# Recurrent attention and MLP mixer on one core: last-row decays by small transfers, batch 0 loaded by SP, state parts behind scores, last outputs kept in PSUM, and a new instruction order

## The chip, the cores and the metric

The kernel runs on one core of a Trainium2 chip. A core has TensorE (PE, matmuls, its weight loads shown as PEld), VectorE (DVE), ScalarE (ACT), GpSimd (POOL) and SyncE (SP), each with its own program in order. Loads and stores are issued by POOL (software queue, which can also change the type) or by SP (hardware queue), and move on 16 DMA engines that both share. The time is in device microseconds, the median of several executions; lower is better.

## The reference

Four batches, eight heads, 768 positions, head size 48. First a gated recurrence (no softmax), then an MLP mixer over tokens and over channels:

```python
f = 1.0 / (1.0 + np.exp(-f_logit))
for t in range(S):
    state = f[:, :, t, :, None] * state + einsum('bhd,bhe->bhde', k[:, :, t], v[:, :, t])
    y[:, :, t] = einsum('bhd,bhde->bhe', q[:, :, t], state)
x = y.transpose(0, 2, 1, 3).reshape(B, S, H * D)          # 4 x 768 x 384
h = np.maximum(x.transpose(0, 2, 1) @ w_tok1, 0.0) @ w_tok2   # 768 -> 256 -> 768
u = x + h.transpose(0, 2, 1)
out = u + np.maximum(u @ w_ch1, 0.0) @ w_ch2               # 384 -> 1536 -> 384
```

## The kernel before

**Staging.** A batch's 768 positions are six chunks of 128 (b is the batch, c the chunk). All inputs are turned to bf16 except f. Batch 0 is loaded chunk by chunk: f by SP, and k, q and v by POOL, which casts (`load`, L265). Behind them POOL loads the weights (L272), then batch 1 (f whole, k, q and v by chunk, with w_ch2 after chunk 1), then batches 2 and 3 whole.

**Recurrence of a chunk** (`gates`, `attention`). ACT makes L = ln(1 + exp(-f)) in f_sb (L335, L336), copies it to bf16 as Lhi (L337), and DVE or POOL takes the rest, Llo = L - Lhi (L340, L343). PE sums L over the positions with a triangular matrix (L363, L364), and, but for the last chunk, the whole chunk's sum per channel in eight one-column matmuls (L361, L362). ACT makes G = exp(-sum), Gi = exp(sum) and, from the one-column sums, glast, the decay over the whole chunk, with channels on the partitions (L372, L374, L377). DVE makes qh = q G and kh = k Gi (L380, L382). PE transposes both (L393), DVE copies them to qkT (L397). PE makes the scores per head, 48 rows of the array at a time (L407), DVE multiplies by the triangle into AmT (L414). PE makes the state's parts, kh times v, 64 columns of the array at a time (L430); DVE adds them to the state (L437, L440) and multiplies by glast (L442); ACT or POOL copies it to state_bd in bf16. The chunk's output y is qkT times the state of the chunk before (L459) plus AmT times v (L466), in one PSUM bank; it is copied out as x_bf and x_nat (L322, L324). G, Gi, qh, kh, qkT, AmT, glast and state_bd have two buffers, by c mod 2.

**Mixer of a batch** (`mixer`). tok1 (L491) contracts over all six chunks of x_bf, a relu makes h1T (L495), tok2 (L503) gives h, DVE adds it to x_nat (L507), ACT casts to u_bf, PE transposes (L519), DVE copies to uT (L524). Then ch1 (L535) with a relu to zT on ACT or DVE (L545, L547), ch2 (L557), an add (L563), and a store by SP (L566).

**Order.** `Plan` holds every step with its engine or engines, what it needs and makes, its PSUM bank (eight banks, given out by the plan) and a cost. `order` goes through them as a list scheduler: the step that can start first is next, ties by a rank written out by hand (`due`, `ranks`), and the engine is chosen there where a step names two. In gaps of PE over 700 ns before 24 us it puts matmuls on a constant tile (`idle`, L597) that nobody reads. The program of each engine is then fixed.

## Time and profile before

| | |
|---|---|
| time, three runs | 188.21 us median, 187.18 to 188.94 |
| the profiled execution | 187.83 us, its span 186.0 us |
| mean granted TensorE clock | 0.963 |
| loads and stores | 19.95 MB in 88437 packets, mean 107 GB/s |
| software queue, hardware queue | 78720 packets, 92.0% of 16 engines' span; 9696 packets, 11.0% |
| one-column matmuls L361, L362 | x80 and x80 |
| Lhi copies on ACT, L337 | 12.2 us, x24, 522 ns each |
| DVE: AmT, qkT, qh, kh | 682, 684, 350, 352 ns each |
| POOL: issue of a load of a chunk | 0.9 us, x36 by chunk |

The span runs from the first to the last instruction. Engines overlap, so busy times don't add up to it. The page cuts the span in 40 slices and gives each engine's busy share in tenths; PEclk is the share of TensorE's clock that was granted. A busy time of PE counts matmuls that overlap in its pipeline once, while the mean of one is its own duration; what a matmul costs PE is the time from its start to the next start.

### The profile page before, as it was taken

What the parts mean: (1) busy time and instruction counts of PE and PEld (TensorE: products, weight loads), DVE (VectorE), ACT (ScalarE), POOL (GpSimd) and SP (SyncE); (2) the same over time, 40 slices, a digit from 0 to 9 for tenths busy, and PEclk for the clock granted to TensorE, in tenths of its full rate; (3) what the DMA queues carried; (4) which work ended last, traced back from release to release, by engine and by line L of the source; (5) the groups of instructions that cost most, each with busy time, mean ns of one, the idle gap of its engine ahead of it and who ended that gap; (6) DMA issues with size and microseconds to landing.
All of it is one profiled execution on the core that took longest, in us unless ns stands there. A gap on an engine that the chain in (4) does not pass through costs nothing.

```text
span 186.0 us, 4513 instructions
## 1 busy us (share of the span) xinstructions
PE 175.5 (94%) x1783; PEld 110.5 (59%) x1783; DVE 130.1 (70%) x296; ACT 127.1 (68%) x309; POOL 66.0 (35%) x78
## 2 busy tenths in 40 slices
PE   6879896899999999999999999999999999999992
PEld 2347573556666656666665666666666666665660
DVE  5388885849998999999988848867686628300222
ACT  5799865699974499999999836557874116698000
POOL 7999993275692444504621501011011000000000
PEclk9995559999999999999999999999999999999999
DMA  8999999999999999999991211011000121110132
GB/s 104 138 169 153 162 210 247 185 159 196 142 118 249 179 162 169 247 201 105 79 125 5 81 49 42 4 42 48 0 0 5 65 73 34 42 42 0 46 127 85
DMA packets 88437, 19.95 MB, mean 107 GB/s; under 512 B 81152, under 2 KB 87600, under 8 KB 88416
## 3 DMA queue, kind: packets, MB, share of 16 engines
q0 software_dynamic: 78720, 13.77, 92.0%
q1 hardware_dynamic: 9696, 5.90, 11.0%
q8 instruction: 14, 0.23, 0.6%
q14 instruction: 7, 0.06, 0.1%
HBM read 25.17 MB, written 4.72 MB: 161 GB/s over the span
## 4 chain that ended last, share of the span: by engine, by line
PE 81%; POOL 5%; DMA 4%; ACT 4%; DVE 3%; issue 2%; POOLq 0%; DVEq 0%
PE ps L535 26%; PE ps L557 25%; PE ps L393 5%; PE ps L491 4%; PE ps L407 4%; DMA v_sb<-in_v_dram 4%; PE ps L503 3%; PE ps L466 2%; PE ps L430 2%; PE ps L519 2%; POOL q_sb L265 2%; PE ps L363 2%; ACT u_bf L322 2%; PE ps L364 1%; PE ps L459 1%
## 5 line engine op out<-in xcount | busy, mean ns | idle before, releaser
L557 PE MATMUL ps<-w_ch,zT 128*128 128x384 bf16 x288 | 54.1, 326 | 0.0
L535 PE MATMUL ps<-uT,w_ch 128*128 128x384 bf16 x288 | 52.6, 326 | 0.0
L545 ACT ACTIVATE zT<-ps 128x384 bf16<-128x384 f32 x76 | 36.5, 490 | 8.3 <-PE ps L535 7.9
L557 PEld LDWEIGHTS <-zT 128*128 128x128 bf16 x288 | 26.8, 98 | 16.5
L535 PEld LDWEIGHTS <-w_ch 128*128 128x128 bf16 x288 | 26.3, 98 | 15.9
L414 DVE TENSOR_TENSOR AmT<-ps,tri_bf 128x512 bf16<-128x512 f32 x48 | 30.6, 682 | 5.3 <-PE ps L407 5.2
L563 DVE TENSOR_TENSOR x_nat<-x_nat,ps 128x384 f32<-128x384 f32 x24 | 13.2, 550 | 22.9 <-PE ps L557 22.5
L265 POOL DMA_DIRECT2D q_sb<-in_q_dram x14 | 15.3, 1095 | 13.6 <-issue 5.2
L322 ACT ACTIVATE x_bf<-ps 128x384 bf16<-128x384 f32 x20 | 9.9, 495 | 12.3 <-PE ps L466 12.1
L265 POOL DMA_DIRECT2D k_sb<-in_k_dram x14 | 15.5, 1105 | 7.6 <-DMA f_sb<-in_f_logit_dram 4.5
L397 DVE COPY qkT<-ps 128x1024 bf16<-128x1024 bf16 x24 | 16.3, 684 | 0.7 <-PE ps L393 0.7
L372 ACT ACTIVATE G<-ps 128x384 bf16<-128x384 f32 x24 | 11.8, 490 | 7.3 <-PE ps L364 7.2
L265 POOL DMA_DIRECT2D v_sb<-in_v_dram x14 | 15.4, 1099 | 3.8 <-issue 2.4
L507 DVE TENSOR_TENSOR x_nat<-x_nat,ps 128x384 f32<-128x384 f32 x24 | 11.5, 547 | 4.1 <-PE ps L503 4.1
L322 ACT ACTIVATE u_bf<-x_nat 128x384 bf16<-128x384 f32 x24 | 11.4, 522 | 4.1 <-DVE x_nat L507 4.1
L326 POOL CAST state_bd<-state 48x192 bf16<-48x192 f32 x10 | 3.4, 344 | 29.8 <-DVE state L442 24.3
L335 ACT ACTIVATE f_sb<-f_sb 128x384 f32<-128x384 f32 x24 | 12.0, 523 | 2.7 <-DMA f_sb<-in_f_logit_dram 2.6
L547 DVE TENSOR_SCALAR zT<-ps 128x384 bf16<-128x384 f32 x20 | 10.4, 552 | 3.7 <-PE ps L535 3.6
L322 ACT ACTIVATE state_bd<-state 48x192 bf16<-48x192 f32 x30 | 10.8, 360 | 3.0 <-DVE state L442 2.6
L491 PE MATMUL ps<-x_bf,w_tok 128*128 128x384 bf16 x48 | 11.9, 330 | 1.0 <-ACT x_bf L322 1.0
L337 ACT ACTIVATE Lhi<-f_sb 128x384 bf16<-128x384 f32 x24 | 12.2, 522 | 0.3
L336 ACT ACTIVATE f_sb<-f_sb 128x384 f32<-128x384 f32 x24 | 12.1, 521 | 0.2
(61 smaller groups left out, 275.8 us busy)
## 6 DMA issues: line engine op xcount, KB each, us to landing
out_dram<-x_nat SPq DMA_DIRECT2D x24, 192.0 KB, 1.9
f_sb<-in_f_logit_dram POOLq DMA_DIRECT2D x3, 1152.0 KB, 10.8
f_sb<-in_f_logit_dram SPq DMA_DIRECT2D x6, 192.0 KB, 4.0
k_sb<-in_k_dram POOLq DMA_DIRECT2D x12, 96.0 KB, 6.6
q_sb<-in_q_dram POOLq DMA_DIRECT2D x12, 96.0 KB, 6.1
v_sb<-in_v_dram POOLq DMA_DIRECT2D x12, 96.0 KB, 6.1
w_ch<-in_moe_w_ch_dram POOLq DMA_DIRECT2D x2, 576.0 KB, 10.4
w_ch<-in_moe_w_ch_dram POOLq DMA_DIRECT2D x1, 1152.0 KB, 14.9
```

The costliest lines, as they stand in the source:

```text
L265: add(engine, 0.0, lambda eng=eng, into=into, of=of: eng.dma_start(out=into, in_=of), make=[(n, b % NB, j) for j in (range(NCH) if c is No ...
L322: nc.scalar.activation(out_, in_, AF.Copy, bias=0.0, scale=1.0)
L335: add(ACT, r, lambda: nc.scalar.activation(fb, fb, AF.Exp, bias=0.0, scale=-1.0), make=[key], kind=el)
L336: add(ACT, r, lambda: nc.scalar.activation(fb, fb, AF.Ln, bias=1.0, scale=1.0), make=[key], kind=el)
L337: add(ACT, r, lambda: nc.scalar.activation(hi, fb, AF.Copy, bias=0.0, scale=1.0), need=[key], make=[lk], kind=el)
L397: add(DVE, r, lambda: nc.vector.tensor_copy(qkT[i], turned()), make=[("qkT", i)], bank=p_t, kind=("el", 1024, True, 2))
L414: add(DVE, r, lambda p=p: nc.vector.tensor_tensor(AmT[i][:, 4 * p:4 * p + 4, :], banks[p_a[p].at].rearrange("s (hp t) -> s hp t", t=C), tb ...
L491: add(PE, rank("tok1", rt), lambda rt=rt, kt=kt, pm=pm: nc.tensor.matmul(banks[pm.at][:, 0:DM], lhsT=w_tok1[:, kt, rt * 128:(rt + 1) * 128 ...
L535: nc.tensor.matmul(banks[pm.at][:, 0:384], lhsT=w[:, kt, c0:c0 + 128], rhs=uT[:, kt, cols], start=(kt == 0), stop=(kt == 2))
L545: nc.scalar.activation(zT[:, cc, cols], banks[pm.at][:, 0:384], AF.Relu, bias=0.0, scale=1.0)
L557: nc.tensor.matmul(banks[pm.at][:, 0:DM], lhsT=zT[:, kt, tt * 128:(tt + 1) * 128], rhs=w_ch2[:, kt, :], start=(kt == 0), stop=(kt == 11))
L563: add(DVE, rank("ch2", tt), lambda un=un, pm=pm: nc.vector.tensor_tensor(un, un, banks[pm.at][:, 0:DM], ALU.add), make=[("x_nat", xn, tt)] ...
```

## The change

- glast of batches 1 to 3 is no longer computed. G is now fp32 and stored with the channels in the order of the partitions, four head pairs innermost; SP copies its last row (position 127 of the chunk) to glast with a transfer of 2 KB per chunk, which spreads one partition's row over 128. The one-column matmuls and their Exp stay in batch 0 alone.
- L is written by the Ln as fp32 into a tile of its own, and Lhi is no copy but the upper halves of its words, read with a step of two bf16 elements. f_sb has two buffers, not three.
- k, q and v of batch 0 come by SP as fp32 into tiles that are free until later (zT and the third x_nat); q and k are multiplied from there, on DVE or POOL, and v is cast by POOL or ACT. POOL's first weight load waits until chunk 4's q has landed (`seen`). The loads of batches 2 and 3 are added to the plan after the gates of batches 0 and 1.
- In batch 0 the transposed q and k have a bank each and are copied by halves on DVE or ACT; the second half of AmT is copied by ACT and masked by POOL (but for the last chunk); Llo and the state copies may go to POOL.
- The state's parts directly follow the scores of their chunk on PE (`tail_of`).
- y of batch 0's chunks 3 to 5 stays in its PSUM bank, tok2 adds to it there, and u_bf and x_nat are both copied from the bank.
- h1T's relu, and copies of batch 0, may go to ACT or DVE.
- The order: steps can ask for a reserve of banks (`room`), PE's gaps over 330 ns get filler matmuls, PE is reckoned at half speed before 5.7 us, and a table of some 300 entries sets rank and lag of single steps.

In the program that comes out, PE has 40 one-column matmuls instead of 160 and 20 filler matmuls instead of 15, seven of them before its first sums instead of 13. POOL's program in batch 0 holds a v cast, then products, Llo, masks and state copies, a second v cast, the two w_tok loads, one more product, two masks and a state copy, and then w_ch1 and batch 1.

```diff
+LEAD = 4000.0
+SHIFTS = (
+    (20,90,800), (25,120,400), (29,150,1600), (46,200,1800), (74,30,100), (75,30,200), (79,60,700), (91,-91,0),
...
+KEPT = 3
 
...
+        op.room = room
+        if tail_of is not None:
+            while tail_of is not None:
+                tail_of.before |= op.before - {tail_of}
+                tail_of.tail = tail_of.tail or op
+                tail_of = next((x for x in self.ops if x.tail is tail_of), None)
...
         if what == "mm":
-            return n[0], n[0] + 166
+            return n[0], n[-1] + 166
...
+    def best(self, *args):
+
+
+        for n, rank, lag in SHIFTS:
+            self.ops[n].rank, self.ops[n].lag = rank / 10, float(lag)
+        return self.order(*args)[1]
...
+                t = max(t, wire - LEAD)
...
+            if follow:
+                t = free[PE]
+                if follow.bank.at is None:
+                    t = max(t, min(banks) + 55)
+                best = ((t, 0.0, t), PE, follow)
...
-                        t = max(t, min(banks) + 55)
-                    if best is None or (t, op.rank) < best[0]:
-                        best = ((t, op.rank), e, op)
-            (t, _), e, op = best
+                        t = max(t, sorted(banks)[op.room - 1] + 55)
+                    key = (t + op.lag, op.rank, t)
+                    if best is None or key < best[0]:
+                        best = (key, e, op)
...
-            if e == PE and free[PE] < until and t - free[PE] > 700:
-                n = int((t - free[PE] - (250 if free[PE] else 1300)) / 430)
-                fill = Op((PE,), 0.0, lambda n=n: idle(n), (), (), None, ("fix", 0, 0))
+            if e == PE and t < cold:
+                own, till = 2 * own, till + own
+            if e == PE and free[PE] < until and t - free[PE] > 330:
+                n = int((t - free[PE] - 1300) / 430) if not free[PE] else int((t - free[PE]) * 0.7 / 220)
+                fill = Op((PE,), 0.0, lambda n=n: idle(n), (), (), None, ("fill", n))
...
+            follow = op.tail
...
-    f_sb = [st([128, H, NCH, D], FP32, f"f_sb{i}") for i in range(NB)]
-    Lhi = [st([128, NCH, H, 64], BF16, f"Lhi{i}") for i in range(2)]
-    Llo = [st([128, NCH, H, 64], BF16, f"Llo{i}") for i in range(2)]
-    G = [st([128, H, D], BF16, f"G{i}") for i in range(2)]
+    f_sb = [st([128, H, NCH, D], FP32, f"f_sb{i}") for i in range(2)]
+    pad = (64, D)
+    L = [st([128, NCH, H, pad[i]], FP32, f"L{i}") for i in range(2)]
+    Lhi = [t.bitcast(BF16).rearrange("t c h (d two) -> t c h d two", two=2)[:, :, :, :, 1] for t in L]
+    Llo = [st([128, NCH, H, pad[i]], BF16, f"Llo{i}") for i in range(2)]
+    G = [st([128, 128, HP], FP32, f"G{i}") for i in range(2)]
+    Gv = [t.rearrange("t (par d) hp -> t hp par d", par=2) for t in G]
...
+    def load_first(n, c):
+        if n == "f":
+            into, src = f_sb[0][:, :, c, :], f_logit
+        else:
+            into, src = first[n][:, c], names[n][1]
+        of = src[0].rearrange("h (c t) d -> t h c d", t=C)[:, :, c, :]
+        add(SP, 0.0, lambda: nc.sync.dma_start(out=into, in_=of),
+            make=[("f", 0, c) if n == "f" else (n, "first", c)], kind=("load", 490, 0, 800))
+        if n == "v":
+            op = add((POOL, ACT), c * 3.0, None,
+                     need=[("v", "first", c)], make=[("v", 0, c)], kind=("el", DM, False, 1))
+            op.fn = lambda: copy_on(op.engine, v_sb[0][:, :, c, :], first["v"][:, c])
...
     def load_w(name, dst, src, size):
-        add(POOL, 0.0,
+        add(POOL, 20.0,
             lambda: nc.gpsimd.dma_start(out=dst, in_=src.rearrange("(kt p) n -> p kt n", p=128)),
-            make=[name], kind=("load", 900, 1024, size))
+            need=["seen"], make=[name], kind=("load", 900, 1024, size))
...
+    load_first("f", 0)
+    load_first("f", 1)
+    for n in "kqv":
+        load_first(n, 0)
+    for c in range(1, NCH):
+        if c + 1 < NCH:
+            load_first("f", c + 1)
+        for n in "kqv":
+            load_first(n, c)
...
+    add(POOL, 0.0, lambda: nc.gpsimd.tensor_copy(seen[:, 0:1], first["q"][:, 4, 0, 0:1]),
+        need=[("q", "first", 4)], make=["seen"], kind=("fix", 100, 100))
...
-    load("fkqv", 2)
...
+        key, whole, rest = ("f", b % 2, c), ("L", b % 2, c), ("Llo", b % 2, c)
-        add(ACT, r, lambda: nc.scalar.activation(fb, fb, AF.Ln, bias=1.0, scale=1.0), make=[key], kind=el)
-        add(ACT, r, lambda: nc.scalar.activation(hi, fb, AF.Copy, bias=0.0, scale=1.0),
-            need=[key], make=[lk], kind=el)
+        add(ACT, r, lambda: nc.scalar.activation(full, fb, AF.Ln, bias=1.0, scale=1.0), need=[key], make=[whole], kind=el)
+        on = (DVE if c < 2 else (DVE, POOL)) if b == 0 else DVE if b < 3 else POOL
+        op = add(on, r, None, need=[whole], make=[rest], kind=("el", DM, False, 1.2))
+        op.fn = lambda: (nc.vector if op.engine == DVE else nc.gpsimd).tensor_tensor(lo, full, hi, ALU.subtract)
...
-            if not last:
+            if b == 0 and not last:
...
-        add(ACT, r, lambda: nc.scalar.activation(G[i], sview(), AF.Exp, bias=0.0, scale=-1.0),
+        add(ACT, r, lambda: nc.scalar.activation(
+            Gv[i][:, :, :, 0:D], pairs(sview()), AF.Exp, bias=0.0, scale=-1.0),
             make=[("G", i)], bank=p_s, kind=el)
...
-        if not last:
+        if b == 0 and not last:
...
+        elif not last:
+            add(SP, r, lambda: nc.sync.dma_start(out=glast[i], in_=G[i][127:128]),
+                need=[("G", i)], make=[("glast", i)], kind=("fix", 490, 2700))
...
+        for out_, in_, by, key, held in (
+                (pairs(qh[i][:, :, 0:D]), pairs(q_c), Gv[i][:, :, :, 0:D], ("qh", i), [("q", at, c), ("G", i)]),
+                (kh[i][:, :, 0:D], k_c, Gi[i], ("kh", i), [("k", at, c), ("Gi", i)])):
+            op = add((DVE, POOL) if b == 0 else DVE, r, None, need=held, make=[key],
+                     kind=("el", DM, False, 1.2 if b == 0 else 1 if key[0] == "qh" else 2))
+            op.fn = lambda op=op, o=out_, x=in_, y=by: times(op.engine, o, x, y)
...
+        if b == 0:
+            for p in range(2):
+                op = add((DVE, ACT), r, None, make=[("qkT", i, p)], bank=p_t[p], kind=("el", 512, True, 2))
+                op.fn = lambda op=op, p=p: copy_on(
+                    op.engine, qkT[i][:, 4 * p:4 * p + 4, :].rearrange("p n t -> p (n t)"),
+                    banks[p_t[p].at].bitcast(BF16)[:, 0:512])
...
+        one = add(PE, r, lambda: None, need=[("qkT", i, 0), ("qkT", i, 1)], bank=p_a[0], kind=("mm", 1), room=2 if last else 3)
+        two = add(PE, r, scores, need=[("qkT", i, 0), ("qkT", i, 1)], bank=p_a[1], kind=("mm", 423 if last else 324, 324), tail_of=one)
...
+            if b == 0 and p == 1 and not last:
+                add(ACT, r, lambda half=half, made=made: nc.scalar.activation(
+                    half, made(), AF.Copy, bias=0.0, scale=1.0),
+                    make=[("AmT", i, p)], bank=p_a[p], kind=("el", 512, True, 1))
+                add(POOL, r, lambda half=half: nc.gpsimd.affine_select(
+                    out=half, in_=half, compare_op=ALU.is_ge, fill=0.0, base=0,
+                    pattern=[[0, 4], [1, C]], channel_multiplier=-1),
+                    make=[("AmT", i, p)], kind=("fix", 760, 760))
...
-            add(PE, r, parts, need=[("kh", i), vk], bank=p_d, kind=("mm", 210))
+            add(PE, r, parts, need=[("kh", i), vk], bank=p_d, kind=("mm", 315, 215), tail_of=two)
...
-                op = add(ACT if b <= 2 else POOL, r, None, need=["state"], make=[("sbd", i, cols.start)],
+                op = add(((POOL, ACT), ACT, (ACT, POOL), POOL)[b], r, None, need=["state"], make=[("sbd", i, cols.start)],
...
-        for tl, key in ((x_bf[b % 2], ("x_bf", b % 2, c)), (x_nat[b % 3], ("x_nat", b % 3, c))):
-            op = add(ACT if b == 0 else (ACT, DVE), r, None, make=[key], bank=p_y, kind=el)
+        if b == 0 and c >= KEPT:
+            kept[c] = p_y
+        for tl, key in ((x_bf[b % 2], ("x_bf", b % 2, c)), (x_nat[b % 3], ("x_nat", b % 3, c)))[
+                :1 if b == 0 and c >= KEPT else 2]:
+            op = add((ACT, DVE), r, None, make=[key], bank=p_y, kind=el)
...
-            add(ACT, rank("tok1", rt), lambda rt=rt, pm=pm: nc.scalar.activation(
-                h1T[:, rt, :], banks[pm.at][:, 0:DM], AF.Relu, bias=0.0, scale=1.0),
-                make=[("h1T", rt)], bank=pm, kind=("el", DM, True, 1))
+                    need=["w_tok1", ("x_bf", xb, kt)], bank=pm, kind=mms(DM), room=4)
+            op = add((ACT, DVE), rank("tok1", rt), None, make=[("h1T", rt)], bank=pm, kind=("el", DM, True, 1))
+            op.fn = lambda op=op, rt=rt, pm=pm: relu(op.engine, h1T[:, rt, :], banks[pm.at][:, 0:DM])
...
-            pm, un = Bank(), x_nat[xn][:, tt, :]
-
-            def tok2(tt=tt, pm=pm):
+            un, held = x_nat[xn][:, tt, :], b == 0 and tt in kept
+            pm = kept[tt] if held else Bank()
+
+            def tok2(tt=tt, pm=pm, held=held):
                 for kt in range(2):
                     nc.tensor.matmul(banks[pm.at][:, 0:DM], lhsT=w_tok2[:, kt, tt * 128:(tt + 1) * 128],
-                                     rhs=h1T[:, kt, :], start=(kt == 0), stop=(kt == 1))
+                                     rhs=h1T[:, kt, :], start=(kt == 0 and not held), stop=(kt == 1),
+                                     skip_group_check=held)
...
+            if held:
+                for tl, key in ((u_bf[:, tt, :], ("u_bf", tt)), (un, ("x_nat", xn, tt))):
+                    op = add((ACT, DVE), rank("tok2", tt), None, make=[key], bank=pm, kind=("el", DM, True, 1))
+                    op.fn = lambda op=op, tl=tl, pm=pm: copy_on(op.engine, tl, banks[pm.at][:, 0:DM])
+                continue
...
     for b in range(B):
         for c in range(NCH):
             gates(b, c, due(b, c) - 3.0)
+        if b < 2:
+            load("fkqv", b + 2)
         for c in range(NCH):
             attention(b, c, due(b, c))
-        if b == 0:
-            load("fkqv", 3)
         mixer(b, ranks(b))
...
-    for op in plan.order(idle, 24000.0):
+    for op in plan.best(idle, 5700.0, 23500.0):
...
```

## The prediction

> **What bounds the kernel now.** I read the page's busy lines first, to see which engine is full, and where.
>
> ```profile
> span 186.0 us, 4513 instructions
> PE 175.5 (94%) x1783; PEld 110.5 (59%) x1783; DVE 130.1 (70%) x296; ACT 127.1 (68%) x309; POOL 66.0 (35%) x78
> ...
> PE   6879896899999999999999999999999999999992
> ...
> PEclk9995559999999999999999999999999999999999
> DMA  8999999999999999999991211011000121110132
> ```
>
> PE is full from the eighth slice to the last. Before that it has gaps and three slices at half clock, and the transfers stay busy to the 21st slice (98 us). Next the table of stretches, for the share of each engine by stage (columns: length, then PE, weight loads, DVE, ACT and POOL busy with counts, granted clock, transfers):
>
> ```profile
> 6.10:30.40 24.30, 20.64 (x261) 13.73 (x259) 20.41 (x45) 19.35 (x51) 22.45 (x28) 0.72 1.92 176
> ...
> 46.50:93.00 46.50, 46.26 (x571) 30.31 (x570) 44.36 (x104) 39.58 (x104) 23.00 (x14) 1.00 1.95 165
> ```
>
> Up to 30.4 (batch 0's recurrence) no engine is idle, but PE runs at 0.72 of its clock; from 46.5 PE is at 99%, with DVE at 95% behind it. The chain of waits says what ended each part:
>
> ```profile
> 12.22 6.90 DMA v_sb<-in_v_dram
> ...
> 32.70 0.34 PE ps L503
> 33.06 0.57 DVE x_nat L507
> 33.65 2.85 ACT u_bf L322 x6
> ...
> 37.12 6.34 PE ps L535 x39
> ...
> 170.75 11.71 PE ps L557 x72
> 182.56 0.55 DVE x_nat L563
> ```
>
> Batch 0's loads, then the hand-over from token to channel mixing, then only PE from 36.95 to 182.56 (145.6 us), then 3.4 us for the last add and store. So the change can gain in two places: what comes before 36.95, and the PE work behind it. Last, PE's order of time, where a start minus the start before it is what a group costs the engine:
>
> ```profile
> 93.17 0.65 PE L535 MATMUL ps<-uT,w_ch 128*128 128x384 bf16 x3
> 93.75 0.40 PE L407 MATMUL ps<-qkT 48*128 48x128 bf16 x8
> 94.08 1.15 PE L535 MATMUL ps<-uT,w_ch 128*128 128x384 bf16 x6
> 95.06 0.17 PE L361 MATMUL ps<-ones_bf,Lhi 128*128 128x1 bf16 x1
> ...
> 95.24 0.16 PE L362 MATMUL ps<-ones_bf,Llo 128*128 128x1 bf16 x1
> 95.27 0.32 PE L363 MATMUL ps<-Lhi,tri_bf 128*128 128x384 bf16 x1
> ```
>
> A channel matmul costs 162 ns; the three at 93.17 hold 580, so entering the scores (48 rows of the array) costs 95. The eight one-column matmuls cost 95.27 - 95.06 = 0.21 us, not the 1.3 us that their durations add to.
>
> **Part 1, decays by small transfers.** The one-column matmuls go from 15 chunks: 15 x 0.21 = 3.1 us off a full PE, a plain gain. The same 15 lose an ACT Exp of 0.18 us, which nobody waits for. In exchange SP moves 2 KB per chunk. No such transfer is in this trace. The nearest: a store by SP lands in 1.9 us with the software queue idle (median from 113 us on), and in 3.5 to 7.5, median 4.6, from 50 to 90 us beside software loads; it moves 96 times the bytes. I take 3 us, between them and nearer the first, since most of a 192 KB store is its own bytes. What waits: the state update on DVE, and on ACT the Exp that refills the same G buffer two chunks later. In the changed order the state is wanted 11 or more us of PE work after its sums in batch 1, and on ACT at least 3.6 us of work lies between the two Exp. SP works in order, and some of the transfers stand behind stores that wait for DVE's last add; the add is then late only if PE is. So 3 us is hidden: nothing.
>
> **Part 2, scores next to state parts.** The parts (L430) use half the columns, and entering them costs too: transposes at 98.10 hold 0.33 us ahead of parts, those at 99.17 0.22 ahead of channel work. Run right behind the scores, one leave and one entry fall together. The trace has it once, at half clock (19.16): the step from parts to scores took 160 ns, as from parts to full-size work there. I take one entry, 95 ns, on each of 15 chunks: 1.4 us (bounds 0 and, if the leave goes too, 2.8). What becomes late is the state, by the wait for the scores; its slack is above.
>
> **Part 3, the split of f.** ACT's 24 copies into Lhi go (12.2 us busy); matmuls read the upper halves of fp32 words instead. At 162 ns to start the next, L363 could cost nothing or twice that for 18 chunks, 2.9 us; I take 0, as every other matmul of this width costs 162 whatever its tile. qh now multiplies by an fp32 G: 0.47 us (the fp32 row L340, start to start) instead of 0.21 to 0.27, on DVE, 24 times; some relus and mask products leave DVE for that.
>
> **Part 4, batch 0 by SP.** The 18 loads of k, q, v leave POOL's queue (0.87 us of issue each, packets of 29 ns) for SP's, where a packet takes 15 ns: the two f loads alone on the rings moved 1479 packets from 2.25 to 3.5 us, so 0.87 us for a load of 1024. 24 loads end near 2 + 24 x 0.87 + 0.8 = 23.7 us, against 23.2 for the last v now; chunk 3's v comes at 17.7, not 19.1. That is no gain at the end of the queue, up to 2 us in its middle. POOL is free for a share of the casts, products and masks. By counts of the new order and start-to-start costs, DVE's work on batch 0 falls from 18.9 to 17.1 us (AmT 12 to 7 at 0.60, kh 6 to 1, Llo 6 to 4 at 0.47, qkT from 6 at 0.60 to 9 halves at 0.33; qh up by 0.23 each, 5 copies of y at 0.46 come in), ACT's by some 2. The last tok1 is at 31.8 now with DVE busy nearly all the way; I take it 2 us earlier (0 to 5: a clock that stays full would free more).
>
> **Part 5, last y in PSUM.** Three of six tiles lose the add (0.46) ahead of the cast, relus of h1T go side by side (0.39 off), copies are shared. The hand-over from the last tok1 to the first channel matmul is 36.95 - 31.8 = 5.2 us, of which 2.0 is tok2 and 1.0 transposes. I take 1.1 off (0.4 to 2).
>
> **Part 6, weights behind batch 0.** The first weight load is issued when chunk 4's q has landed: 20 loads, 2 + 20 x 0.87 + 0.8 = 20.2, against 18.3 now. From there to batch 2's v took 58.0 us (18.3 to 76.3). So that v lands at 78.3, and f of batch 1, 37.8 now, near 39.7. With channel work from 33.8 the first sums of batch 1 are due 7.8 us of PE work later at 41.6, f and its gates (1.7) are there at 41.4; batch 2's first parts are due 36.0 later, 77.6. This slack was 3 us and is gone: I put 1.0 on for it.
>
> **Sum.** Channel work starts at 36.95 - 2.0 - 1.1 = 33.8. PE behind it 145.6 - 3.1 - 1.4 = 141.1, plus 1.0 for loads, plus 3.4: span 179.3. The profiled run took 187.83 with a span of 186.04, so 1.8 around it: 181.1. It lies 0.4 below the median of 188.21, so I give **181.5**.
>
> **Rivals.**
>
> *The clock stays low* (0.12). It fell at 13.4 after two windows in which the array streamed about 0.4 of the time, and rose at 27.0 after one at 0.83. There are now 7 opening filler matmuls, not 13, so the early rise may fail; but 13 stand in later gaps, not 2. If batch 0 gains nothing: 36.95 + 141.1 + 1.0 + 3.4 + 1.8 + 0.4 = 184.7.
>
> *POOL and DVE hinder each other* (0.05). POOL gets about 13 us of batch 0's elementwise work. In the trace its Llo takes 910 to 921 ns, but 1026 when it began 0.26 us before a DVE Llo ended. If 15 DVE steps with two SBUF inputs each wait half a POOL step (0.45) six times in ten, DVE loses 4 us: 185.5. The Trainium skill, SBUF — State Buffer, section "SBUF: two separate sides", says that the two share a port pair under an exclusive lock, held for a whole instruction. The 1026 agrees with it.
>
> *G's layout is slow* (0.07). G is now written and read with a step of 16 bytes; no row has one. Were each element to cost twice, six qh of batch 0 put 2.4 us on DVE, ten more 4 us on a DVE that has 2.1 idle between 46.5 and 93: 2.4 + 1.9, so 185.8. The Trainium skill, SBUF — State Buffer, section "Door 1: The DMA port swizzle (why `[64,N]` ≈ `[32,N]`)", speaks for it: lines are 16 bytes, and an access that goes to a new line each time pays. No run here shows it yet.
>
> *Loads become the bound* (0.14). At 1063 packets per us (the second from 2 to 3 us) 20 loads end at 22.1, and POOL must pass masks and state copies of chunks 3 and 4 before it issues w_ch1, up to 2 us. Then batch 2's v is 4 us later still: +4 to 5, up to 186.5.
>
> *The small transfers are late* (0.10, slower). Beside software loads stores took up to 7.5 us. Past 3.6 to 4.5 us ACT stands at the refill of G, with zT evictions queued behind, and PE runs out of banks. At 6 us that is 2 us on each of 8 refills in batches 1 and 2: 181.5 + 16 = 197; it ends above 190 from about 5.3 us on. For it: the stores' 4.6. Against it: their size.
>
> **Numbers.** The forecast has 0.52: 177 to 184.5 (front 2 us better or worse, entry saving 0 to 2.8, strided Lhi at worst). Faster by over 1% (about what a measurement here can tell from no change) is under 186.3: the forecast, the low clock, the hindrance, half of the layout and a third of the loads, 0.52 + 0.12 + 0.05 + 0.035 + 0.05, so 0.77. The rest of those two is within 1%, 0.13; slower 0.10. The range, 176.5 to 188.5, leaves out most of the late transfers and a front over 2 us better.
>
> **What would show it.** Right: first channel matmul near 34, first sums of batch 1 near 41, no one-column matmuls behind it, PE at 99% from there to 175, small transfers landing in under 3.6 us. Wrong: ACT waiting on transfers ahead of G, PE waiting for v or f, half clock past 20 us, a G row well over 490 ns.

## The result and the profile after

The kernel after takes 195.5 us (median of 4 runs, 194.18 to 196.15) where the kernel before took 188.15 beside it (4 runs, 187.18 to 188.94): slower by 3.8%, ratio 1.0384, 95% interval 1.0307 to 1.0461. The forecast was 181.5. The profiled run took 195.02, its span is 193.3 us where the sum had 179.3. So 14.0 us are to be found in the profile. Where some runs of a kernel fell in a slower state of the chip (tied_all, before_view, row_exp), its time below is the median of the others.

The page after, its busy lines and slices:

```profile
span 193.3 us, 4276 instructions
PE 175.4 (91%) x1668; PEld 107.6 (56%) x1668; DVE 139.4 (72%) x291; ACT 121.0 (63%) x259; POOL 68.3 (35%) x87
...
PE   6697869799969999989599999999999999999992
...
PEclk9997975999999999999999999999999999999999
DMA  6999997999999999999999911011000003120132
```

DVE is busy 9.3 us longer, and ACT only 6.1 us less, though the 24 copies into Lhi (12.2 us) and 15 small Exp are gone. PE, full from its eighth slice on before, has a 6, an 8 and a 5 in its 12th, 18th and 20th. The table of stretches (columns: length, then PE, weight loads, DVE, ACT and POOL busy with counts, granted clock, transfers) for the same 50 us, first of the kernel after:

```profile
48.00:98.00 50.00, 43.97 (x472) 27.48 (x471) 44.99 (x93) 39.36 (x87) 23.67 (x17) 1.00 1.92 170
```

and of the kernel before:

```profile
48.00:98.00 50.00, 49.75 (x617) 32.38 (x614) 47.03 (x109) 42.79 (x112) 23.78 (x15) 1.00 1.96 161
```

PE stands 6.0 us of these 50, at full clock, and no other engine is full either: it is waits that pass from engine to engine. The chain of waits, from the hand-over to channel mixing on (start, length, what):

```profile
34.95 0.57 DVE h1T L445
35.56 0.50 PE ps L650 x2
...
39.52 4.40 PE ps L688 x27
...
50.47 0.76 ACT G L489
51.25 4.48 DMA glast<-G
55.81 0.85 ACT G L489
...
90.06 4.74 DMA glast<-G
94.82 0.85 ACT G L489
95.69 0.86 DVE qk L448
96.60 1.07 PE ps L515 x16
...
178.15 11.71 PE ps L705 x72
```

Two things are new in it. The small transfer stands on the chain, twice, and each time what it releases is the Exp of G, not the state: the Exp writes the G buffer that the transfer reads. At 94.82 one sees all of it: the transfer lands, ACT makes G, DVE makes qh from it, PE transposes qh, and PE had nothing to do for 2.14 us. And the first channel matmul comes at 39.4, not at 33.8 (36.95 before), the last one ends at 189.9: 150.5 us of PE time where the sum had 142.1 with the loads' share. So 5.6 of the 14.0 us are lost in front of the channel work, 8.4 behind it. The groups that changed their length (columns: busy, mean ns of one, idle time before them), G and qh:

```profile
L489 ACT ACTIVATE G<-ps 128x384 f32<-128x384 f32 x24 | 20.6, 868 | 5.6 <-DMA glast<-G 2.8 <-DVE qk L448 1.4 <-PE ps L481 1.3
...
L448 DVE TENSOR_TENSOR qk<-q_sb,G 128x384 bf16<-128x384 bf16 x18 | 15.2, 847 | 2.5 <-ACT G L489 2.5
...
L448 DVE TENSOR_TENSOR qk<-zT,G 128x384 bf16<-128x384 f32 x6 | 6.7, 1123 | 1.8 <-ACT G L489 1.6 <-DMA zT<-in_q_dram 0.2
```

The last line is qh of batch 0, where q comes as fp32. G took 490 ns before and every qh 350. The last view of the kernel after is that of the transfers by SP from 45 to 100 us (how many, KB each, median us from issue to landing):

```profile
out_dram<-x_nat SPq DMA_DIRECT2D x6, 192.0 KB, 4.6
...
glast<-G SPq DMA_DIRECT2D x8, 2.0 KB, 4.6
```

2 KB take as long as 192 KB. From 100 us on, where the software queue is almost idle, both take 1.9.

### The profile page after: what moved, and what is told of

It reads as the page before. It is cut to its first block, busy times and chain, and to the rows that moved or that the text cites. A ratio compares the mean times of both kernels' runs of the same rounds, so it can differ in the third digit from the quotient of the medians.

```text
span 193.3 us, 4276 instructions
## 1 busy us (share of the span) xinstructions
PE 175.4 (91%) x1668; PEld 107.6 (56%) x1668; DVE 139.4 (72%) x291; ACT 121.0 (63%) x259; POOL 68.3 (35%) x87
## 3 DMA queue, kind: packets, MB, share of 16 engines
q1 hardware_dynamic: 30576, 9.47, 20.4%
## 4 chain that ended last, share of the span: by engine, by line
PE 61%; ACT 14%; DVE 11%; DMA 6%; POOL 3%; issue 3%; ACTq 0%; POOLq 0%
PE ps L705 22%; PE ps L688 15%; DMA glast<-G 5%; PE ps L515 5%; DVE qk L448 4%; ACT G L489 4%; PE ps L638 4%; PE ps L537 3%; PE ps L650 2%; ACT L L458 2%; ACT f_sb L457 2%; PE ps L608 2%; PE ps L601 2%; ACT zT L443 2%; PE ps L672 2%
## 5 line engine op out<-in xcount | busy, mean ns | idle before, releaser
L515 PE MATMUL ps<-ident,qk 128*128 128x128 bf16 x192 | 19.3, 233 | 8.3 <-DVE qk L448 7.2
L489 ACT ACTIVATE G<-ps 128x384 f32<-128x384 f32 x24 | 20.6, 868 | 5.6 <-DMA glast<-G 2.8
L515 PEld LDWEIGHTS <-qk 128*128 128x128 bf16 x192 | 13.4, 103 | 17.4 <-DVE qk L448 12.7
L438 POOL CAST state_bd<-state 48x192 bf16<-48x192 f32 x22 | 8.9, 402 | 32.8 <-DVE state L584 21.1
L448 DVE TENSOR_TENSOR qk<-q_sb,G 128x384 bf16<-128x384 bf16 x18 | 15.2, 847 | 2.5 <-ACT G L489 2.5
L378 POOL DMA_DIRECT2D q_sb<-in_q_dram x8 | 9.8, 1220 | 13.0 <-issue 5.1
L378 POOL DMA_DIRECT2D k_sb<-in_k_dram x8 | 9.8, 1220 | 9.5 <-DMA f_sb<-in_f_logit_dram 4.8
L457 ACT ACTIVATE f_sb<-f_sb 128x384 f32<-128x384 f32 x24 | 12.0, 519 | 1.7 <-DMA f_sb<-in_f_logit_dram 1.7
L492 ACT ACTIVATE Gi<-ps 128x384 bf16<-128x384 f32 x24 | 12.3, 511 | 1.0 <-PE ps L481 1.0
L458 ACT ACTIVATE L<-f_sb 128x384 f32<-128x384 f32 x24 | 12.3, 519 | 0.3
## 6 DMA issues: line engine op xcount, KB each, us to landing
f_sb<-in_f_logit_dram POOLq DMA_DIRECT2D x3, 1152.0 KB, 12.2
```

The source lines that it names most:

```text
L378: add(engine, 30.0, lambda eng=eng, into=into, of=of: eng.dma_start(out=into, in_=of), make=[(n, i, j) for j in (range(NCH) if c is None e ...
L448: (nc.vector if eng == DVE else nc.gpsimd).tensor_tensor(out_, in0, in1, ALU.mult)
L457: add(ACT, r, lambda: nc.scalar.activation(fb, fb, AF.Exp, bias=0.0, scale=-1.0), make=[key], kind=el)
L458: add(ACT, r, lambda: nc.scalar.activation(full, fb, AF.Ln, bias=1.0, scale=1.0), need=[key], make=[whole], kind=el)
L489: add(ACT, r, lambda: nc.scalar.activation(Gv[i][:, :, :, 0:D], pairs(sview()), AF.Exp, bias=0.0, scale=-1.0), make=[("G", i)], bank=p_s, ...
L515: nc.tensor.transpose(to[:, o + hp, :], blk(src)[:, hp, :], ident)
```

## The experiments

Two theories were tried against each other first: G's step of 16 bytes (theory 1), and the small transfers ahead of the Exp (theory 2); a third, the front, came after. All times are beside the kernel before on the same chip (187.7 to 188.7 there). Where a run keeps the order of a kernel, each engine's program is the same but for the edit; where the planner sets it anew, the text says so. The first channel matmul and the PE time from it to PE's end are from the profiled run.

| run | time, us | against before, 95% | first channel matmul | PE behind it |
|---|---|---|---|---|
| before | 188.2 | 1 | 36.95 | 145.5 |
| after | 195.50 | 1.031 to 1.046 | 39.36 | 150.5 |
| strided_sums | 193.15 | 1.022 to 1.030 | 39.16 | 149.2 |
| flat_sums | 190.01 | 1.005 to 1.018 | 37.27 | 148.2 |
| four_G | 190.92 | 1.012 to 1.018 | 38.85 | 146.7 |
| before_strided | 199.04 | 1.055 to 1.061 | 40.30 | 153.3 |
| flat_four | 194.04 | 1.023 to 1.038 | 36.91 | 152.1 |
| flat_two | 205.24 | 1.083 to 1.098 | 36.98 | 162.9 |
| row_exp | 198.49 | 1.046 to 1.056 | 36.74 | 157.5 |
| front_flat | 190.82 | 1.009 to 1.021 | 37.24 | 147.5 |
| flat_dve | 191.18 | 1.013 to 1.021 | 38.49 | 147.8 |
| v_by_pool | 192.33 | 1.016 to 1.028 | 38.86 | 147.8 |
| tied_later | 190.67 | 1.011 to 1.019 | 36.93 | 148.3 |
| tied_all | 191.74 | 1.015 to 1.025 | 38.41 | 148.4 |
| before_view | 189.14 | 1.003 to 1.009 | | |
| keep_tied | 191.74 | 1.015 to 1.023 | 36.64 | 149.4 |
| keep_view | 188.18 | 0.997 to 1.003 | 37.19 | 145.5 |
| keep_both | 192.10 | 1.016 to 1.024 | 37.01 | 149.9 |
| hand_front | 201.09 | 1.065 to 1.077 | 39.14 | 157.0 |
| untied_front | 211.47 | 1.118 to 1.134 | 39.58 | 165.7 |

### The transfer and the layout, one at a time

strided_sums gives the one-column matmuls back to batches 1 to 3 and takes the transfers out:

```diff
-            if b == 0 and not last:
+            if not last:
                 bh, bl = blk(hi_c), blk(lo_c)
...
+        def decay():
+            nc.scalar.activation(glast[c % 4], banks[p_s.at][:, DM:DM + HP], AF.Exp, bias=0.0, scale=-1.0)
...
+            nc.scalar.activation(Gi[i], sview(), AF.Exp, bias=0.0, scale=1.0)
+            if b and not last:
+                decay()
```

> The kernel after, in its own order, with one thing undone: glast of batches 1 to 3 comes from one-column matmuls and an Exp again, not from a transfer; G keeps its step of 16 bytes. Theory 1 (the layout of G costs most: its Exp takes 868 ns for 490 and qh 847 for 350, in front of batch 0 and on a full DVE): only the waits that a transfer ends go, at most 5 us, and 3.1 us of matmuls come back: 192.5 to 195, first channel matmul still near 39.5. Theory 2 (the late transfers cost most: 4.0 to 4.7 us where 3 were reckoned, in front of the refill of G): nearly all of the 9.7 us that PE stands behind 39.5 go, and 3.1 come back: 188 to 190.5, first channel matmul near 39.5.

193.15: 2.35 below the kernel after, within theory 1's band. If the one-column matmuls cost the 3.1 us that the prediction took for them, the transfers cost some 5. (L of odd batches gets the padding to 64 columns that these matmuls need. In this run and in flat_sums batch 2's last decay is overwritten by batch 3's first, as they share a buffer, so batch 2's last chunk gets a wrong state; the instructions and their order are the same with five buffers, which flat_dve, v_by_pool, hand_front and untied_front have.)

flat_sums takes G back to bf16 in a row as well, so it undoes the step and the fp32 together:

```diff
-    G = [st([128, 128, HP], FP32, f"G{i}") for i in range(2)]
-    Gv = [t.rearrange("t (par d) hp -> t hp par d", par=2) for t in G]
+    G = [st([128, H, 64], BF16, f"G{i}") for i in range(2)]
+    Gv = [t.rearrange("t (hp par) d -> t hp par d", par=2) for t in G]
```

> As strided_sums, and G is bf16 with heads and channels in a row again, as before the change. Theory 1 (layout): the G row is back at 490 ns, qh at 350 (fp32 q of batch 0 some 550), batch 0 gains about 3 us on DVE and ACT, so the first channel matmul is near 36.5, and PE no longer stands behind it: 185 to 187.5. Theory 2 (transfers): within 1.5 us of strided_sums. Theory 3 (the front is late by its loads and its order): the first channel matmul stays past 38.5 whatever the layout.

190.01, 3.1 below strided_sums: between the theories, above the 187.5 of the first. The first channel matmul comes 1.9 us earlier, PE's part is 0.9 shorter. With everything undone that the two theories name, the kernel is still slower than before.

four_G leaves both in place and gives G four buffers, so that no Exp waits for a transfer:

```diff
-        i, nb = c % 2, b % NB
+        i, nb, g = c % 2, b % NB, c % 4
...
-            Gv[i][:, :, :, 0:D], pairs(sview()), AF.Exp, bias=0.0, scale=-1.0),
+            Gv[g][:, :, :, 0:D], pairs(sview()), AF.Exp, bias=0.0, scale=-1.0),
```

> The kernel after, in its own order, with four G buffers for two, by c mod 4: no Exp waits for the transfer of the G before the last; layout and transfers stay. Theory 2 (transfers, by that wait on ACT): the stalls near 54, 56 and 94.5 us go, 187 to 190. Theory 1 (layout): DVE's longer products hold PE in the same stretch, 192 to 195.5. If the state's wait for glast on DVE is what counts, nothing changes: 195 to 196.

190.92, 4.6 below the kernel after, by one index: just above theory 2's band, below theory 1's. The eight transfers up to 100 us still take 4.2 to 5.0 us from issue to landing; only the wait of ACT is gone. The same 50 us as above:

```profile
48.00:98.00 50.00, 47.48 (x507) 29.56 (x506) 48.50 (x100) 42.85 (x95) 27.20 (x21) 1.00 1.99 175
```

PE is back from 43.97 to 47.48, and now DVE is the full engine, 48.50 of 50, and what PE waits for most behind the first channel matmul is DVE's products qh and kh (1.5 us, five times): that is theory 1.

before_strided is theory 1 by itself, in the kernel before:

```diff
-    G = [st([128, H, D], BF16, f"G{i}") for i in range(2)]
+    G = [st([128, 128, HP], FP32, f"G{i}") for i in range(2)]
+    Gv = [t.rearrange("t (par d) hp -> t hp par d", par=2)[:, :, :, 0:D] for t in G]
```

> The kernel before, in its own order, with nothing but G's layout of the change: fp32, a step of 16 bytes from channel to channel. Theory 1 (layout): Exp near 870 ns, qh near 850; 0.49 us more on DVE for each of six chunks ahead of the first channel matmul and some ten behind it where DVE was 95% busy: 192 to 197, first channel matmul 39 to 41. Theory 2 (transfers): the layout alone is hidden, 188 to 190.

199.04, 11 us more than before, from a layout alone, above what theory 1 had. Its groups:

```profile
L376 ACT ACTIVATE G<-ps 128x384 f32<-128x384 f32 x24 | 20.7, 861 | 7.8 <-PE ps L368 7.7
L384 DVE TENSOR_TENSOR qh<-q_sb,G 128x384 bf16<-128x384 bf16 x24 | 20.3, 847 | 4.9 <-ACT G L376 4.7
```

24 x 0.50 = 11.9 us more on DVE and 24 x 0.37 = 8.9 on ACT. 3.4 us of it come out ahead of the first channel matmul, 7.8 behind it. In front the granted clock may have a part too: it is half from 10.9 to 31.3 us in this profile, from 13.4 to 27.0 in that of the kernel before.

### Both undone without the one-column matmuls

flat_four puts the fp32 row in order and keeps four buffers; a row in that order needs four transfers to reach the partitions:

```diff
-            add(SP, r, lambda: nc.sync.dma_start(out=glast[i], in_=G[i][127:128]),
+            add(SP, r, lambda: [nc.sync.dma_start(out=glast[i][:, hp:hp + 1], in_=G[g][127:128, 2 * hp:2 * hp + 2, :]) for hp in range(HP)],
```

> The kernel after, in its own order, with four G buffers and G as fp32 with heads and channels in a row; glast still by transfers, now four per chunk (one for each head pair, 512 bytes each), since one can't turn that row. The layout and the wait of the Exp for the transfer are both undone, and no one-column matmuls come back. Theory (the two costs add: 4.6 us from four_G, 3.2 from strided_sums to flat_sums): 187.5 to 188.5, first channel matmul 37 to 37.5. Rival (the four transfers are late by SP's 1.9 us of issue, and the state with them): 190 or more.

194.04, not 188: the rival. The front is 2.4 us better than the change's, but the four transfers land 5.0 us after their issue at the median (36 of them, 45 to 105 us) and the issues are 0.6 us apart, so a chunk's last one is there some 7 us after G. Now the state on DVE waits for it, with qkT's copy queued behind, and PE stands 2.9 us for that copy (to 73.6). The clock adds to it: it is half from 73.0 to 79.8 us, where PE is busy 6.2 us with what full clock does in half the time. So up to 3.1 of the 5.4 us between this PE time and four_G's are the clock, and the profile can't say whether the wait brought that about. flat_two is the same with two buffers:

> As flat_four, with two G buffers as in the change: the layout alone is undone, the Exp still waits for the transfers. Theory: 195.5 - 3.2 = 192.3, or up to 1.5 more, as the last of four transfers lands later; ACT's waits for transfers ahead of G as long as in the kernel after or longer. Rival (with short products and Exp the waits are the same ones, counted twice): 190 to 191.

205.24, far outside: with the transfers longer, the wait of the Exp costs 11.2 us (flat_two against flat_four), not 4.6. It isn't the clock: both profiles have 6.8 us at half clock behind the first channel matmul. The groups of flat_two:

```profile
L489 ACT ACTIVATE G<-ps 128x384 f32<-128x384 f32 x24 | 11.7, 490 | 14.9 <-DMA glast<-G 12.1 <-DVE state L579 1.4 <-PE ps L481 1.3
L448 DVE TENSOR_TENSOR qk<-q_sb,G 128x384 bf16<-128x384 bf16 x18 | 9.8, 549 | 4.1 <-ACT G L489 4.0
```

ACT stands 12.1 us for transfers (2.8 in the kernel after), with G's Exp back at 490 ns. The line also parts the two halves of theory 1: fp32 in a row costs ACT nothing and DVE 549 for 350; the step costs ACT 378 more and DVE 298.

row_exp writes the strided row by an Exp of its own over 32 positions:

```diff
+            if b and not last:
+                nc.scalar.activation(Gsv[c % 4][96:128, :, :, 0:D], pairs(sview())[96:128], AF.Exp, bias=0.0, scale=-1.0)
```

> The kernel after, in its own order: G is bf16 in a row again, and a second Exp over the last 32 positions alone writes the fp32 row with the step of 16 bytes into one of four small tiles, from which the transfer goes as in the change. So no product reads the step, no Exp waits for a transfer, batch 0 has no strided write, and no one-column matmuls come back; ACT pays some 0.65 us for each of 15 chunks. Theory (layout and the Exp's wait are what the change lost behind 39.5, the front takes 2 of the rest): first channel matmul 37 to 37.5, 187 to 188.5. Rival (the state's own wait for the transfers holds PE, as in flat_four): 190 or more.

198.49: the first half of the theory holds (first channel matmul 36.74), the second falls, though not by the rival's mechanism: behind the first channel matmul no step of DVE waits for a transfer of glast, while PE waits for ACT's Gi (1.6 us), the extra Exp (1.2) and L (0.8). So the run measures the price of the extra Exp. I had put it at 0.65 us; it takes as long for 32 positions as for 128:

```profile
L494 ACT ACTIVATE Gs<-ps 32x384 f32<-32x384 f32 x15 | 12.9, 858 | 0.3
```

With it ACT is busy 14.93 of the 17 us from 40 to 57, where batch 1's gates are due, and PE 13.36; then the granted clock falls to half from 56.9 to 63.7. What a kernel with neither cost would take was therefore not measured. flat_sums less 3.1 us of one-column matmuls puts it near 187, an estimate that takes all of the 3.1 as gain.

### The front

flat_dve takes kh and the second half of AmT from POOL (and ACT) to DVE in batch 0 of flat_sums:

```diff
-            op.fn = lambda op=op, o=out_, x=in_, y=by: times(op.engine, o, x, y)
+            op.fn = lambda op=op, o=out_, x=in_, y=by: times(DVE, o, x, y)
```

> flat_sums (with a fifth glast buffer, so that batch 2's last decay is its own), in its order, with kh of batch 0 on DVE, not POOL (0.91 us there), and the second half of AmT by one DVE product, not by an ACT copy and a POOL select. Theory (POOL's share lengthens the chain of batch 0: 0.91 for 0.55, and 0.6 + 0.63 for 0.68, and both hinder DVE's products beside them): first channel matmul 35 to 36.3 for 37.3, 187.5 to 189. Rival (DVE becomes the bound of batch 0): 37.3 or later, 190 or more.

191.18, first channel matmul 38.49, 1.2 us later: my theory fell and its rival stands. DVE is busy 23.1 of the 27.9 us from 6 us to the last tok1 there, for 19.8 of 26.7 in flat_sums, so POOL's share helps. That POOL hinders DVE is seen all the same. In flat_sums DVE's products of batch 0, in order of time:

```profile
14.91 1.15 DVE L448 TENSOR_TENSOR qk<-zT,G 128x384 bf16<-128x384 f32 x1
...
19.56 0.99 DVE L448 TENSOR_TENSOR qk<-zT,G 128x384 bf16<-128x384 f32 x1
...
23.43 0.55 DVE L448 TENSOR_TENSOR qk<-zT,G 128x384 bf16<-128x384 f32 x1
```

and POOL's beside them:

```profile
14.82 0.82 POOL L461 TENSOR_TENSOR Llo<-L 128x384 bf16<-128x384 f32 x1
...
19.10 1.03 POOL L560 TENSOR_SCALAR_AFFINE_SELECT AmT<-AmT 128x512 bf16<-128x512 bf16 x1
```

The third, while POOL does nothing but issue a load (22.81 to 24.54), takes 0.55. The first two, begun while POOL computes, take twice that, and each ends 0.41 us after POOL's instruction.

v_by_pool gives batch 0's v back to POOL's queue, in flat_sums, and the casts of v go:

```diff
+        if n == "v":
+            issue = lambda: nc.gpsimd.dma_start(out=v_sb[0][:, :, c, :], in_=of)
```

> flat_sums (five glast buffers), in its order, with batch 0's v loaded and cast by POOL again, so that SP issues 18 loads for batch 0, not 24, and the casts of v go. Theory (SP's loads, 0.9 us apart, set the end of batch 0): last q lands 3 us or more earlier and the first channel matmul at 34.5 to 36. Rival (batch 0 is a chain over ACT, DVE and POOL, its loads are not what it waits for): 36.8 or later, and 189 to 191.5.

192.33, first channel matmul 38.86. The premise did not come true: with 18 loads on SP instead of 24 the last q landed at 26.2, not 3 us before flat_sums' 25.4. SP's issues, 0.8 us each there, took up to 2.6. The last v came earlier, at 22.8 for 28.4, so the 24 loads as a whole ended at 26.2 for 28.4; q did not gain from it, and whether an earlier q would help the front was not tried. The profiles do correct a term of the prediction: by SP, q of chunk 5 lands at 24.7 in the kernel after, by POOL it landed at 22.7 before.

front_flat is four_G with G in a row for batch 0 alone:

```diff
+        gv = Gv[g][:, :, :, 0:D] if b else pairs(G0[i])
```

> four_G, in the order of the kernel after, with G of batch 0 alone as bf16 in a row (batch 0 needs no transfer); batches 1 to 3 keep the step of 16 bytes and the transfers. Theory (batch 0 loses some 2 us by the strided G, and what comes earlier there stays earlier to the end): first channel matmul 36.7 to 37.3 for four_G's 38.85, 188.5 to 189.5. Rival (batch 1 then waits for its loads, and the front's gain is lost there): 190.3 to 191.

The front gains 1.6 us as expected, the time nothing that can be told (190.82 against 190.92): the rival. Batch 1's f lands at 43.6 there, 44.1 in the kernel after, so the sums of batch 1 wait for it however early the channel work begins (ACT's first Exp of that f stands 0.8 us for the load in front_flat, and not in the kernel after).

### Parts 2 and 3 alone

tied_later and tied_all bind the parts to the scores in the kernel before, and the planner sets the order anew:

```diff
+        def both():
+            scores()
+            if tied:
+                parts()
...
-        two = add(PE, r, scores, need=[("qkT", i)], bank=p_a[1], kind=("mm", 270))
+        two = add(PE, r, both, need=[("qkT", i), *more], bank=p_a[1], kind=("mm", 380 if tied else 270))
```

> The kernel before, with the state's parts right behind the scores of their chunk in batches 1 to 3 alone (15 chunks); batch 0 and the hand-written ranks as they were, the planner sets the rest. Theory (one entry of the array saved per chunk, 95 ns): 15 x 0.095 = 1.4 us less, 186.3 to 187.2; the step from the scores to the parts is 146 to 150 ns and no 95 are paid ahead of the parts. Rival (the state is late by the wait for the scores, PE stands): 188 to 190.

> As tied_later, and in batch 0 too. Theory (batch 0 is a chain from state to state, and the parts now wait for transposes, their copy and the scores): the states of batch 0 come 1 to 2 us later and the first channel matmul with them, 38 to 39, so 187.5 to 189.5. Rival (the state has slack in batch 0 too): five more entries saved, 186 to 187.

190.67 and 191.74. The first is the rival and a little past it, 2.8 us more of PE time. The second is as its theory said at the front, 38.41 against 36.93, and not in the time (187.5 to 189.5 there). Nor is the 1.5 us the late states alone: the first state comes 3.4 us later (13.72 for 10.37), but the last tok1 only 0.5 (32.03 for 31.57). The other 1.0 lies in the hand-over to channel mixing, where the clock is half from 33.1 to 36.5 in tied_all and full in tied_later (tok2's twelve matmuls take 3.96 us for 2.33). keep_tied leaves the order alone and moves the parts, the state's add, its product and its copies of 11 chunks behind the scores:

```diff
+            late = [x for x in group if seq.index(x) < at]
...
+            for x in late:
+                seq.remove(x)
+            at = seq.index(scores)
+            seq[at + 1:at + 1] = late
```

> The kernel before, in its own order, with the parts, the state's add and its copies of 11 chunks of batches 1 to 3 moved behind the scores of their chunk, and nothing else moved (tied_later let the planner set everything anew). Theory (95 ns per chunk, and tied_later lost it by its new order): 11 x 0.095 = 1.0 us less, 186.8 to 187.3. Rival (the later state itself makes PE stand): 188.5 to 190.

191.74: the rival again, past its 190. The saving is there, and is lost elsewhere. PE of keep_tied at one chunk, scores and parts:

```profile
54.55 0.40 PE L408 MATMUL ps<-qkT 48*128 48x128 bf16 x8
54.88 0.31 PE L431 MATMUL ps<-v_sb,kh 128*64 128x48 bf16 x8
```

The last scores start 146 ns before the parts, a plain leave, with no 95 on top, as in the kernel after. But DVE's waits for the parts, of keep_tied

```profile
DVE tsum L441 <- PE ps L431: 7.3, 9, 1.3
```

and of the kernel before (us in total, times, longest)

```profile
DVE tsum L440 <- PE ps L430: 1.0, 2, 0.5
```

DVE works in order: it comes to the state's add before PE comes to the parts, and everything behind the add waits too.

before_view leaves ACT's copies into Lhi out and reads the upper halves (the planner sets the order anew); keep_view does so in the order of before; keep_both is keep_view with keep_tied:

```diff
+    L = [st([128, NCH, H, 64], FP32, f"L{i}") for i in range(2)]
+    Lhi = [t.bitcast(BF16).rearrange("t c h (d two) -> t c h d two", two=2)[:, :, :, :, 1] for t in L]
...
-        add(ACT, r, lambda: nc.scalar.activation(hi, fb, AF.Copy, bias=0.0, scale=1.0),
+        add(ACT, r, lambda: None,
```

> The kernel before, with L as fp32 in its own tile, and Lhi as the upper halves of its words, no copy on ACT (f_sb has two buffers, the loads of batch 2 follow the gates of batch 0 in the plan, as in the change). Theory (the view costs PE 9 ns for 18 sums and takes 24 x 0.52 us off ACT, of which one copy stood ahead of every sums of batch 0): first channel matmul 0.5 to 1 us earlier, 186.5 to 187.8. Rival (ACT's copies were hidden): 188 to 188.5.

> The kernel before, in its own order, with the Lhi copies left out and the upper halves of L's fp32 words read in their place (two f buffers). before_view without a new order. Theory: PE pays 9 ns for 18 sums, ACT loses 12 us of work that stood in front of batch 0's sums: first channel matmul 0.3 to 1 us earlier, 187.2 to 188. Rival (the copies were hidden): 188 to 188.5.

> keep_tied and keep_view in one: the two parts of the change that cost nothing by the trace, in the order of before. Theory: the two gains add, 186.3 to 187.2, the fastest of all kernels here. Rival: 188 or more.

189.14, 188.18 and 192.10. before_view is above both of its bands, in an order set anew. In the order of before the view changes nothing (ratio 1.000, interval 0.997 to 1.003): the copies were hidden, and the strided read costs little. keep_both is keep_tied. No kernel here beats the kernel before.

hand_front is flat_sums with the table of ranks left out for batch 0's recurrence, untied_front lets its parts run ahead of the scores besides; both are planned anew:

```diff
-        for n, rank, lag in SHIFTS:
+        for n, rank, lag in [x for x in SHIFTS if x[0] >= 279]:
...
-            add(PE, r, parts, need=[("kh", i), vk], bank=p_d, kind=("mm", 315, 215), tail_of=two)
+            add(PE, r, parts, need=[("kh", i), vk], bank=p_d, kind=("mm", 315, 215), tail_of=two if b else None)
```

> flat_sums (five glast buffers) with the table of ranks and lags used from batch 0's mixer on alone; batch 0's recurrence goes by the hand-written ranks. The control for untied_front. If the searched order of batch 0 was worth something on the chip: first channel matmul later than 37.3, 191 or more; if not: 189 to 190.5.

> hand_front with batch 0's state parts free to run before the scores again. Theory (as tied_all against tied_later, 1.5 us at the first channel matmul): 1 to 2 us ahead of hand_front there and in the whole. Rival (the states of batch 0 have slack in this kernel): within 0.7 us of hand_front.

201.09 and 211.47, and untied_front fits neither its theory nor its rival. Its states of batch 0 do come earlier (the last at 28.6 for 30.9), and yet the first channel matmul is 0.4 later. The tie can't be read from these two: the whole order moved with it, and most of the loss is behind the first channel matmul (157.0 and 165.7), where the same part of the table was in force. What they show is that the table holds only for the order that it was made on.

## Why the prediction was wrong

**Part 1, the transfers: the largest of three steps that failed.** "I take 3 us, between them and nearer the first, since most of a 192 KB store is its own bytes", and so "3 us is hidden". The nearest row was the other one: 2 KB land 4.6 us after issue beside the software queue, as 192 KB do. The Trainium skill, SBUF — State Buffer, section "The DMA setup-cost knee (why "@ 1 MiB" ≠ asymptote)", says that a transfer pays about 2 us whatever its size. The 1.9 us for both sizes from 100 us on agree with it; the 4.6 beside software loads are more than it gives. The wait for the Exp costs 4.6 us (four_G). The rival "the small transfers are late" had the mechanism and the place, the Exp ahead of zT's evictions. That its 197 is near the 195.5 is luck: it had 16 us for that wait, four_G shows 4.6, and the layout and the front, which it left at their forecast, made up the rest. It set the point from which it decides at 5.3 us and gave it 0.10. But ACT waits already where the transfer lands later than ACT's work lasts: the profile has two such waits, of 1.3 and 1.5 us, behind 3.7 and 3.0 us of work between the two Exp, where "at least 3.6" was reckoned, and the second leaves PE without work for 2.14. What the state's own wait costs was put at nothing on a slack of 11 us; in the kernel after that held, in flat_four, with landings some 2.5 us later, it did not.

**The layout: a rival of 0.07 that came true.** Its price, 185.8, was 4.3 us on the forecast; in the change's order the step and the fp32 together cost 3.1 (strided_sums against flat_sums), so the size was about right there, though the step with fp32 costs 11 in the order of before. The chance was too low: no row spoke against the doubling. The forecast's own term for it, "0.47 us (the fp32 row L340, start to start)" for qh and nothing for the Exp, came from a row that reads fp32 in a row: the trace had no row with a step, and the bounds should have held the double. The "0.23 each" for qh of batch 0 in Part 4 went with it: those six take 1.12 us, and 0.80 in flat_sums, for 0.36 before. The Trainium skill, SBUF — State Buffer, section "Door 1: The DMA port swizzle (why `[64,N]` ≈ `[32,N]`)", says that SBUF has lines of 16 bytes and that each access to a new line pays. 549 to 847 ns on DVE and 490 to 868 on ACT for the same elements with a step of 16 bytes agree.

**Part 4, the front: no gain at all.** The last tok1 was to start at 29.8; it starts at 34.75, and at 32.1 to 32.7 where G is in a row (31.6 before). The five kernels with G of batch 0 in a row and POOL's share kept (flat_sums, flat_four, flat_two, row_exp, front_flat) have the first channel matmul at 37.0 on average, before had it at 36.95, the sum had 33.8. So 3.2 of the 5.6 us are gains that did not come. The other 2.3 are what the kernel after loses to these five; the two pairs that differ in G's layout and type alone (strided_sums and flat_sums, four_G and front_flat) put 1.6 to 1.9 on it. The fewer steps on DVE were counted in engine time, but batch 0 is a chain, and the count itself did not come true: DVE's work from 6 us to the last tok1 was to fall by 1.8 us, and it is 20.4 us before, 21.3 in the kernel after and 19.8 in flat_sums. Chunk 0's G is ready 1.2 us earlier than before (7.36 against 8.56), but its state 2.3 us later, at 12.47 against 10.16, since its parts now stand behind transposes, copies and scores (with G in a row it comes at 11.5 to 12.7 too): the prediction weighed this wait for batch 1 alone. In the order of before, binding batch 0 moved the last tok1 by 0.5 us. The loads by SP end 2.2 us later than before (last v at 25.4 for 23.2), not 0.5: from the first landing at 3.7 on one lands every 0.94 us, not 0.87. And DVE's products wait for POOL, the rival of 0.05: in flat_sums the six of batch 0 take 0.25 us more on average than the 0.55 of one alone, 1.5 us in all. How the 3.2 us divide between these is not settled.

**The clock** was a rival of 0.12 and, as "half clock past 20 us", a sign. The kernel after has it: half from 16.8 to 20.2 and from 27.0 to 33.8, 10.2 us where before had 13.7. Little of the front hangs on it: flat_four too has 10.2 us at half clock there and flat_two none, and their first channel matmuls come at 36.91 and 36.98. At most the 0.5 us between the kernel after and four_G (half from 28.0 to 31.4 alone, 38.85) may be the second stretch, which is argued, not shown.

**Part 2** was right in its size at PE, 95 ns per chunk (146 from scores to parts, none ahead), and wrong in "its slack is above": alone it makes the kernel before 2.8 to 3.5 us slower. **Part 3** was right for the matmuls: L480 to L481 takes 171 ns for 162, 18 x 9 = 0.16 us, and keep_view is equal to before. **Part 5** was right within its bounds: the hand-over is 39.36 - 34.75 = 4.6 us for 5.4, 0.8 off for 1.1. **Part 6**: f of batch 1 lands at 44.1, not 39.7, since the first weight load is issued at 22.8, not 20.2, and POOL then stays with the last chunks' product, masks and state copy until w_ch1 goes out at 29.5; batch 2's v lands at 85.7, not 78.3. The prediction had this as a rival, "up to 2 us" on POOL; it was 5. In the kernel after this costs PE no wait that the profile shows, as the channel work is late itself.

**The sum.** 14.0 us: in front 3.2 by the missing gains and 2.3 mostly by the layout; behind, 3.8 by the Exp's wait (150.5 to 146.7 in four_G) and 0.9 by the layout (strided_sums to flat_sums). That leaves 3.7, which was not traced to one cause. What PE waits for there differs by kernel: in four_G 1.5 us for qh and kh on DVE, in flat_sums 0.6 for the gates of batch 1 (late f) and 1.9 at one copy of x_nat on DVE. So the sign was lost by several terms, none of which alone would have made the kernel slower than before, and a sum that put the unseen ones at nothing held no reserve for them. Three of the signs named for a wrong prediction are in the profile: ACT waits on transfers ahead of G, G's row is at 868 ns, and the clock is half past 20 us.

## What to carry to other kernels

A step of 16 bytes was paid by both engines that used it, ACT writing and DVE reading, so lay a tile out for the engines that touch it 48 times, not for the transfer that reads one row. The small transfer here was late by the queues beside it, not by its bytes: price one by a large one in the same stretch, and give what it reads more buffers, since the engine that refills it waits as well. Before binding two steps to save an entry, look at which in-order engine has the second one's user already in its program.

## What was not expected of the hardware

- A transfer of 2 KB from SBUF to SBUF by SP lands 4.6 us after issue beside software loads (45 to 100 us), like a store of 192 KB; 1.9 us for both from 100 us on.
- ACT's write with a step of 16 bytes takes 858 ns for 32 positions and 868 for 128: it goes by the elements of a row. In a row it takes 490 in bf16 and in fp32.
- DVE's product of bf16 with fp32 takes 549 ns in a row and 847 with the step; with both in bf16, 350.
- PE's moving operand with a step of two bf16 costs 171 ns for 162.
- DVE's product of batch 0 takes 0.55 us alone and 0.95 to 1.15 where it begins well before the end of a POOL instruction (flat_sums).
- With 6 of 24 loads of 192 KB moved from SP's queue to POOL's, the last of all lands at 26.2 us for 28.4, but the last q at 26.2 for 25.4: SP's issues take up to 2.6 us for 0.8.
- 10.2 us at half clock in batch 0 or none (flat_four, flat_two) give the same first channel matmul, 36.91 and 36.98 us.
